# Loading w_o with four neighbouring rows to a partition in a fused decode layer, forward and backward

## The chip, the cores and the metric

The kernel runs on one core of one Trainium2 chip. The time is the device time of one execution in microseconds (us); the median of several executions is compared. A profile is one more execution, recorded by the hardware; its span is a little shorter than its own time, because start and end of the program lie around it.

## What is computed

One decoder layer with adaptive layer norm, for a single token of width 1024, and its gradients for all inputs. Attention has 32 query heads of 128 on 4 key/value heads and looks at the last 4096 of 65536 cached positions; the feed-forward network (FFN) is a gated unit of width 3584.

```python
mod = (silu(c) @ w_mod)              # sa, ca, ga, sb, cb, gb: six sections of 1024
h = layernorm(x) * (1 + ca) + sa
q = h @ wq                           # 32 heads of 128
p = softmax(q k^T * 128**-0.5)       # last 4096 positions of the cache
o = p v
x = x + ga * (o @ wo)                # wo: (32*128, 1024)
h = layernorm(x) * (1 + cb) + sb
x = x + gb * ((sigmoid(h @ w_gate) * (h @ w_up)) @ w_down)
```

The outputs are x and the gradients of x, k_cache, v_cache, wq, wo, w_gate, w_up, w_down, c and w_mod. The gradients of the two caches are zero outside the last 4096 positions, and writing these zeros is most of the memory traffic: 185.60 MB are written to memory and 78.28 MB read.

## The kernel before, in words

The order of the work is written out by hand; nothing is scheduled by a planner. Each engine runs its own list in order. Transfers are issued by POOL (most of them), by SP (w_down, parts of w_mod, some stores of the end) and, at the start, by ACT. The zeros go out as some 120 pieces of about 1 MB. `zero(n, after)` issues the next n of them on POOL; `after` makes POOL wait for a matmul first, so that the fills are paced by the computation. The lists `Z_...` at the top say how many are issued at which place. `dep` and `recent` only carry these waits.

The stages, with their times in the profile:

- Up to about 72 us: the loads of K, w_q and V, the modulation, q, the scores and the softmax. w_q is transposed into `A_all` (also called `a4[:, j, h, :]`: eight blocks j of 128 input rows, 32 heads h).
- The N loop, 72 to 155 us, line 697. For each of the four groups g of eight query heads it accumulates, over 32 steps t_, a 128x1024 matrix in two PSUM banks (`n_ps`, line 708), from keys times values weighted with p. One DVE product (line 703, in helper line 233) serves two steps, a *pair*. It ends with a rank-1 term (line 726, it needs `bd`, built by ACT in step 20) and two ACT copies into `N_sb` (line 729). At odd steps `side()` runs one waiting job.
- The jobs of groups 1 to 3 are the `t_unit`s (line 660) of the group before: T of head h is `N_sb` of the head, transposed, times the transposed w_q block of the head; two matmuls of 512 columns (line 666) and two copies (line 668) put it back into `a4`. The last eight heads (`tlast`) come after the loop, between the first chunks of b.
- b, 155 to 305 us: `bch()` (line 755) multiplies T of one input block p, four heads at a time, with the four 128-row blocks of one w_o tile `wo_t[u]`: eight matmuls into two banks (line 765). Between them: `attn_units` (o times w_o, line 787), the second layer norm, the folding of w_mod and the first loads of the FFN.
- The FFN, 306 to about 478 us: seven blocks q, each loaded, used for forward and backward, overwritten by its gradient and stored. In its idle moments PE transposes `wo_t` in place (line 1077), for do.
- The end: dattn (the gradient at the attention's output), do = w_o times dattn (line 1188, copied by ACT at line 1190 into `do_sb`, then turned into columns `do_ps` at line 1275), the gradient of w_o (`dwo`, line 1218), and those of w_mod, w_q, V and K.

w_o has 4096 rows: head times 128 plus position d in the head. `wo_t[u]` holds the 512 rows of heads 4u to 4u+3 as four tiles `[:, a, :]` of 128 partitions. In the loads (`wo_dram`, line 371) the tile index a is the head and the partition is d, so one partition takes four rows that are 128 rows apart in memory. In the store of its gradient (`dwo_dram`, line 374) a partition takes four rows that are neighbours. For that store, o is brought into the second order by 16 small fp32 matmuls (`op_ps`, line 1156), copied to `o_perm` (the buffer of `kb_col`), before the last layer norm's backward step.

PSUM has few banks; each pool names its own by a tag: `mm`, `gu`, `x`, `acc`, `pq`, `rq` one each, `na` two. `new_ps()` hands out banks in turn (in the N loop: `mm`, `gu`, `x`), `new_acc()` the bank `acc`.

Of the kernel before, what the change touches and what calls it, by code (L numbers as in the profile page):

```python
# [10 lines left out]
P = 128  # L11
FP32 = mybir.dt.float32
# [12 lines left out]
HQ = 32  # L25
G = 4
HG = HQ // G
DH = 128
# [18 lines left out]
NT = 8  # L47
# [12 lines left out]
def kernel(  # L60
# [26 lines left out]
    nc = tc.nc  # L87
# [3 lines left out]
    psum = ctx.enter_context(tc.tile_pool(name="psum", bufs=1, space=bass.MemoryType.PSUM))  # L91
    pacc = ctx.enter_context(tc.tile_pool(name="pacc", bufs=1, space=bass.MemoryType.PSUM))
    pna = ctx.enter_context(tc.tile_pool(name="pna", bufs=2, space=bass.MemoryType.PSUM))
    pgu = ctx.enter_context(tc.tile_pool(name="pgu", bufs=1, space=bass.MemoryType.PSUM))
    px = ctx.enter_context(tc.tile_pool(name="px", bufs=1, space=bass.MemoryType.PSUM))
# [25 lines left out]
    ident_f = vt([P, P], "ident_f")  # L121
# [96 lines left out]
    def new_ps(name="ps"):  # L218
        p, tag = next_pool()
        return p.tile([P, 512], FP32, name=name, tag=tag)  # L220
# [4 lines left out]
    def new_acc(name="acc"):  # L225
        return new_bank(name)[:, 0:64]
# [14 lines left out]
    def cp(out, a):  # L241
        return nc.vector.tensor_copy(out=out, in_=a)  # L242
# [110 lines left out]
    a4 = A_all.rearrange("p (j h m) -> p j h m", j=KD, h=HQ)  # L353
# [5 lines left out]
    N_sb = ar(144, 8)  # L359
# [6 lines left out]
    wo_t = [ar(o, 8).rearrange("p (a n) -> p a n", a=4) for o in wo_off]  # L366
# [2 lines left out]
    B_t = [junk if o is None else ar(o, 2) for o in B_off]  # L369

    def wo_dram(t, u):
        return t[u * 512:(u + 1) * 512, :].rearrange("(a d) n -> d a n", d=DH)

    def dwo_dram(u):
        return out_5[u * 512:(u + 1) * 512, :].rearrange("(p a) n -> p a n", a=4)

    def load_wo(u, eng=nc.gpsimd):
        eng.dma_start(out=wo_t[u], in_=wo_dram(A_wo, u))
# [123 lines left out]
    jobs = []  # L502
# [26 lines left out]
    for j in range(KD):  # L529
# [6 lines left out]
        for b in range(2):  # L536
            mm = rows_mm(q_ps[b], h1_bf[:, j:j + 1], heads(wq_t[j])[:, 16 * b:16 * b + 16, :], j == 0, j == KD - 1)
# [15 lines left out]
    for ch in range(8):  # L553
        ps = new_ps("sc_ps")
        for g in range(G):
            mm = nc.tensor.matmul(ps[32 * g:32 * g + 32, 0:512], lhsT=q_col2[:, HG * g:HG * g + 32],
                                  rhs=k_T[:, g, ch * 512:(ch + 1) * 512], start=True, stop=True,
                                  tile_position=(0, 32 * g))
# [18 lines left out]
    for tb in range(4):  # L577
        c = slice(tb * 1024, (tb + 1) * 1024)
# [31 lines left out]
    o_col = vt([P, HQ], "o_col")  # L610
    o_bf = vt([P, HQ], "o_bf", BF16)
    kb_col = vt([P, HQ], "kb_col")
# [26 lines left out]
    def ok_rows():  # L639
        cp(o_col, ok_ps[:, 0:HQ])  # L640
        cp(kb_col, ok_ps[:, HQ:2 * HQ])
        cp(o_bf, o_col)
        lo = scr[:, 768:832].bitcast(FP32)
        for k, (col, rows, s) in enumerate(((o_col, o_rows, 1.0), (kb_col, nkb_rows, -1.0))):
            st = st_cols[k].rearrange("p (a h) -> p a h", a=4)
            cp(st[:, 0, :], col)
            tt(lo, col, st[:, 0, :], ALU.subtract)
            cp(st[:, 3, :], lo)
            cp(st[:, 1, :], st[:, 3 - 3 * k, :])
            cp(st[:, 2, :], st[:, 3 * k, :])  # L650
            rp = new_tp("rp_ok")[:, 0:P]
            nc.tensor.transpose(rp, st_cols[k], ident_bf[:, :])
            nc.scalar.activation(out=rows, in_=rp, func=ACT.Copy, scale=s)

    def build_bd(g):
        for i in range(HG):
            nc.scalar.activation(out=bd[:, i, :], in_=o_rows, func=ACT.Copy,
                                 scale=sel[:, HG * g + i:HG * g + i + 1])

    def t_unit(h, engs="AA"):  # L660
        def run():
            for k in range(2):
                j1 = min(4 * k + 4, NT)
                ps = new_ps("t_ps").rearrange("p (j m) -> p j m", j=4)[:, 0:j1 - 4 * k, :]
                o = a4[:, 4 * k:j1, h, :]
                nc.tensor.matmul(ps, lhsT=N_sb[:, h * P:(h + 1) * P], rhs=o, start=True, stop=True)  # L666
                if engs[k] == "A":
                    nc.scalar.copy(out=o, in_=ps)  # L668
                else:
                    cp(o, ps)  # L670
        return run

    jobs.clear()

# [22 lines left out]
    for g in range(G):  # L697
        nbank = bank_pair("n_ps", g)
        for t_ in range(KT):
            s = g * KT + t_  # L700
            vp = vp_t[(s // 2) % 2]
            if t_ % 2 == 0:
                tt(vp.rearrange("p t h d -> p (t h d)"),
                   v_nat[:, g, t_ * DH:(t_ + 2) * DH].rearrange("p (t o d) -> p t o d", t=2, o=1).broadcast_to([P, 2, HG, DH]),
                   pT2[:, g, HG * t_:HG * t_ + 2 * HG, :].rearrange("p n (o k) -> p n o k", o=1).broadcast_to([P, 2 * HG, 64, 2]),
                   ALU.mult)
            for k in range(2):
                mm = nc.tensor.matmul(nbank[k][:, :], lhsT=k_nat[:, g, t_ * DH:(t_ + 1) * DH],  # L708
                                      rhs=vp[:, t_ % 2, 4 * k:4 * k + 4, :].rearrange("p h d -> p (h d)"),
                                      start=(t_ == 0), stop=False)  # L710
            zero(Z_N[s], recent(mm, 6), True)
            if t_ == 20:
                build_bd(g)
            if s == 2:
                ok_cols(ok4)
            elif s == 4:
                ok_rows()
            elif s == 24:
                gb_cols = mod_gb((6, 7))
                load_wo(0)  # L720
            elif s == 26:
                gb_cols()
            elif t_ % 2 == 1:
                side()
        for k in range(2):
            nc.tensor.matmul(nbank[k][:, :], lhsT=nkb_rows[:, :], rhs=bd[:, 4 * k:4 * k + 4, :].rearrange("p h d -> p (h d)"),
                             start=False, stop=True)
            c0 = (HG * g + 4 * k) * P
            nc.scalar.activation(out=N_sb[:, c0:c0 + 512], in_=nbank[k][:, :], func=ACT.Copy, scale=float(SCALE))
        load_wo(4 + g)  # L730
        if g < 3:
            jobs.extend(t_unit(h, "AA") for h in range(HG * g, HG * g + HG))
    load_wo(3)
    side(len(jobs))
    tlast = [t_unit(h, "AV") for h in range(HG * 3, HQ)]


    bq = []
# [36 lines left out]

    for i in range(4):
        bch()
        tlast[2 * i]()
        tlast[2 * i + 1]()
    bch(2)  # L780
    attn_col = vt([P, KD], "attn_col")
    row_sel = vt([P, 1], "row_sel")
# [1 line left out]
    attn4 = [new_ps("attn4") for _ in range(2)]  # L784

    def attn_units(us, first):
        for a in range(4):
            for k in range(2):
                for c in range(4):
                    h = 4 * us[c] + a  # L790
                    nc.tensor.matmul(attn4[k][32 * c:32 * c + 32, :], lhsT=o_bf[:, h:h + 1].broadcast_to([P, 32]),
                                     rhs=wo_t[us[c]][:, a, k * 512:(k + 1) * 512], start=(first and a == 0),
                                     stop=(not first and a == 3), tile_position=(0, 32 * c))

# [87 lines left out]
    v = A3_ps[:, 0:48].rearrange("p (j n) -> p j n", j=KD)  # L882
# [270 lines left out]
    dh2 = vt([P, KD], "dh2")  # L1153
    nc.vector.reduce_sum(out=dh2, in_=dh2acc.rearrange("p (b j) -> p j b", j=KD), axis=AX.X)
    dln2 = vt([P, KD], "dln2")
    op_ps = new_acc("op_ps")
    for hh in range(4):
        for a in range(4):
            nc.tensor.matmul(op_ps[32 * hh:32 * hh + 32, 8 * a:8 * a + 8], lhsT=ident_f[:, a::4], rhs=o_col[:, hh::4],
                             start=True, stop=True, tile_position=(0, 32 * hh))  # L1160
    o_perm = kb_col
    cp(o_perm, op_ps[:, 0:HQ])
    mulv(dln2, dh2, cb1)
    dx1b, m2 = layernorm_bwd_col(dln2, ln2, rstd2, "ln2b")
    dx1 = vt([P, KD], "dx1")
# [16 lines left out]
    do4 = [new_ps("do4") for _ in range(2)]  # L1182
    do_sb = [ar(158, 2).bitcast(FP32), scr.bitcast(FP32)]
    for b in range(2):
        for i in range(KD):
            for a in range(4):
                w = wo_t[4 * b + a].rearrange("p a (i d) -> p i a d", i=KD)
                nc.tensor.matmul(do4[b][32 * a:32 * a + 32, :], lhsT=dattn_bf[:, i:i + 1].broadcast_to([P, 32]),
                                 rhs=w[:, i, :, :], start=(i == 0), stop=(i == KD - 1), tile_position=(0, 32 * a))
        nc.scalar.copy(out=do_sb[b], in_=do4[b][:, :])  # L1190
    dh1_ps = new_acc("dh1_ps")
    for p in range(NBP):
        for it in range(KD):
            nc.tensor.matmul(dh1_ps[:, p:p + 1], lhsT=B_t[p][:, it * P:(it + 1) * P], rhs=dattn_bf[:, it:it + 1],
                             start=(it == 0), stop=(it == KD - 1))
# [22 lines left out]
    def dwo(u):  # L1218
        for a in range(4):
            outer_dve(wo_t[u][:, a, :], o_perm[:, 8 * a + u:8 * a + u + 1], dattn_b)  # L1220
        nc.gpsimd.dma_start(out=dwo_dram(u), in_=wo_t[u])

    def rebuild_P():
        tp = new_tp("tp_P")
# [48 lines left out]
    for b in range(2):  # L1273
        for hh in range(4):
            nc.tensor.matmul(dov[:, b, :, hh], lhsT=do_sb[b][:, hh * P:(hh + 1) * P], rhs=ident_f[:, 0::32],
                             start=True, stop=True)
    for g in range(G):
        tr_unit(N_sb[:, g * 1024:(g + 1) * 1024])()
    for u in (2, 4, 5, 6):
        dwo(u)  # L1280
# [25 lines left out]
    for tc_ in range(4):  # L1306
        nc.tensor.matmul(c_ps[32 * tc_:32 * tc_ + 32, 0:1], lhsT=pd, rhs=ones_f[:, 0:1],
                         start=True, stop=True, tile_position=(0, 32 * tc_))
# [17 lines left out]
    for c2 in range(2):  # L1326
        ps = new_ps("dp_ps")
# [107 lines left out]
```

## Time and profile before

| | |
|---|---|
| median of 3 runs | 594.28 us (593.79 to 594.58) |
| the profiled execution: its own time, its span | 593.98 us, 592.2 us |
| DMA bytes, mean rate over the span | 246.53 MB, 416 GB/s |
| share of DMA time on POOL's queue, on SP's and ACT's | 92.3%, 12.8% |
| packets under 8 KB, all packets | 23712, 37484 |
| 1 MB loads of w_o: number, median from issue to landing | 8, 11.4 us |
| 1 MB loads of w_q: number, median from issue to landing | 8, 20.9 us |
| T matmuls (line 666): number, ns of one | 64, 379 |
| T copies on ACT (line 668): number, ns of one | 56, 588 |

Busy time of an engine is given with its share of the span. A row of the profile's groups reads: line, engine, operation, what it writes <- what it reads, shape, number, then busy time and the mean length of one, then the idle time of the engine just before, with what ended it. Matmuls are pipelined: one of 512 columns is shown as 379 ns long, while the next can start 216 ns later. PEld is the load of a matmul's weights. A transfer's time to landing counts from its issue and includes waiting behind earlier ones. A line of a stretch of time (a window) gives its start and end, its length, the busy time and number of instructions of PE, PEld, DVE, ACT and POOL, the granted TensorE clock, the DMA share and GB/s.

### The profile page before, as it was taken

The page shows a single profiled execution, that of the slowest core. Times are in us where ns is not written, and L with a number is a line of the kernel's source. Part 1 is how long each engine was busy: PE and PEld are TensorE (multiplying, and loading weights), DVE is VectorE, ACT ScalarE, POOL GpSimd, SP SyncE. Part 2 cuts the span into 40 slices and gives each one's busy share as a digit, 9 for nine tenths or more (in the row PEclk, how much of TensorE's full clock was granted, in tenths as well). Part 3 has the DMA queues.
Part 4 walks back from the last instruction along what each step waited for, and adds up shares of the span by engine and source line. Part 5 has one row for each costly group of instructions (what it writes and reads, how often), then busy time and mean ns, then how long its engine had stood idle before and what let it go on. Part 6 is the DMA issues. An engine that isn't in the chain of part 4 may idle for free.

```text
span 592.2 us, 9529 instructions
## 1 busy us (share of the span) xinstructions
PE 397.7 (67%) x3819; PEld 239.4 (40%) x3844; DVE 360.7 (61%) x677; ACT 259.9 (44%) x398; POOL 158.0 (27%) x258
## 2 busy tenths in 40 slices
PE   3997689999899999988866237244262455984030
PEld 2784333334344546534436136234252424631000
DVE  3665599999511020176548685677866878968160
ACT  2579614567311014212135375464654655893020
POOL 3112223212223112222221334223343145222000
PEclk9998699999999999997995565565555568755555
DMA  8999999999999999999999999999999999999998
GB/s 349 420 419 421 412 457 388 464 417 430 426 422 396 431 446 424 432 431 401 421 422 388 417 414 416 409 413 416 416 414 413 419 419 405 419 425 420 422 416 363
DMA packets 37484, 246.53 MB, mean 416 GB/s; under 512 B 6097, under 2 KB 6097, under 8 KB 23712
## 3 DMA queue, kind: packets, MB, share of 16 engines
q0 software_dynamic: 30144, 218.65, 92.3%
q1 hardware_dynamic: 7248, 27.27, 12.8%
q8 instruction: 30, 0.49, 0.3%
q14 instruction: 14, 0.11, 0.1%
q10 hardware_dynamic: 48, 0.01, 0.0%
HBM read 78.28 MB, written 185.60 MB: 446 GB/s over the span
## 4 chain that ended last, share of the span: by engine, by line
DMA 36%; PE 34%; DVE 18%; ACT 5%; issue 4%; ACTq 0%; DVEq 0%; POOLq 0%; POOL 0%; SPq 0%
DMA out_dram<-arena 15%; PE b_ps L765 12%; DMA arena<-in_B_w_down_dram 7%; DMA out_dram<-out_dram 6%; PE n_ps L708 6%; DVE arena L246 5%; DVE arena L250 5%; DMA arena<-in_B_w_gate_dram 5%; DVE arena L233 4%; DMA arena<-in_w_mod_dram 3%; ACT arena L519 2%; PE t_ps L666 2%; PE w_ps L461 1%; PE tp_k L498 1%; PE tp_side L908 1%
## 5 line engine op out<-in xcount | busy, mean ns | idle before, releaser
L765 PE MATMUL b_ps<-arena 128*128 128x512 bf16 x494 | 116.0, 383 | 2.5 <-ACT arena L909 1.1
L909 ACT COPY arena<-tp_side 128x1024 bf16<-128x1024 bf16 x62 | 60.9, 1014 | 71.4 <-PE tp_side L908 71.1
L233 DVE TENSOR_TENSOR arena<-arena 128x2048 bf16<-128x2048 bf16 x64 | 76.5, 1223 | 2.3 <-PE n_ps L708 0.3
L765 PEld LDWEIGHTS <-arena 128*128 128x128 bf16 x512 | 49.2, 99 | 58.7 <-issue 5.3
L250 DVE CUSTOM_DVE_ANT_0 arena<-arena,scr 128x1024 bf16<-128x1024 bf16 x56 | 66.2, 1219 | 9.5 <-ACT scr L1071 9.5
L708 PE MATMUL n_ps<-arena 128*128 128x512 bf16 x249 | 65.2, 378 | 6.2 <-DVE arena L233 4.2
L200 POOL DMA_DIRECT2D out_dram<-out_dram x68 | 33.6, 495 | 116.2 <-PE n_ps L708 37.5
L908 PE MATMUL tp_side<-ident_bf,arena 128*128 128x128 bf16 x496 | 54.9, 289 | 11.6 <-DVE arena L233 5.2
L908 PEld LDWEIGHTS <-arena 128*128 128x128 bf16 x496 | 47.0, 135 | 17.6 <-issue 8.9
L1032 PE MATMUL fg<-h_bf,arena 128*128 128x1 bf16 x448 | 15.6, 166 | 48.3 <-DMA arena<-in_B_w_up_dram 28.8
L708 PEld LDWEIGHTS <-arena 128*128 128x128 bf16 x256 | 24.6, 97 | 41.2 <-issue 15.8
L250 DVE CUSTOM_DVE_ANT_0 arena<-arena,b1k 128x1024 bf16<-128x1024 bf16 x24 | 28.4, 1220 | 20.8 <-PE fg L1050 20.8
L281 ACT ACTIVATE arena<-scr,h 128x1024 bf16<-128x1024 bf16 x35 | 38.6, 1144 | 2.3 <-DVE dh2acc L250 1.5
L206 POOL DMA_DIRECT2D out_dram<-zeros x45 | 25.1, 562 | 54.0 <-PE q_ps L436 15.1
L941 POOL DMA_DIRECT2D out_dram<-arena x28 | 22.1, 793 | 64.4 <-ACT arena L281 45.4
L1255 ACT ACTIVATE arena<-ps_kv 128x512 bf16<-128x512 f32 x48 | 25.0, 723 | 29.7 <-PE ps_kv L1251 29.7
L1251 PE MATMUL ps_kv<-arena 32*128 32x512 bf16 x64 | 23.8, 543 | 19.7 <-DVE arena L246 18.6
L668 ACT CAST arena<-t_ps 128x512 bf16<-128x512 f32 x56 | 30.1, 588 | 12.1 <-PE t_ps L666 12.1
L242 DVE CAST arena<-b_ps 128x512 bf16<-128x512 f32 x6 | 4.1, 691 | 50.4 <-PE b_ps L765 50.4
L1032 PEld LDWEIGHTS <-arena 128*128 128x128 bf16 x448 | 14.0, 105 | 50.9 <-DMA arena<-in_B_w_up_dram 30.4
L519 ACT COPY arena<-tp_wq 128x1024 bf16<-128x1024 bf16 x23 | 21.4, 1071 | 7.3 <-PE tp_wq L517 7.3
L246 DVE TENSOR_SCALAR arena<-arena,cs_col 128x4096 bf16<-128x4096 bf16 (+1 forms) x16 | 16.0, 1014 | 12.3 <-DMA out_dram<-arena 12.3
(314 smaller groups left out, 618.1 us busy)
## 6 DMA issues: line engine op xcount, KB each, us to landing
out_dram<-zeros POOLq DMA_DIRECT2D x45, 1024.0 KB, 14.1
out_dram<-arena POOLq DMA_DIRECT2D x28, 1024.0 KB, 18.5
out_dram<-arena POOLq DMA_DIRECT2D x30, 512.0 KB, 10.9
out_dram<-arena SPq DMA_DIRECT2D x20, 512.0 KB, 9.8
arena<-in_A_wq_dram POOLq DMA_DIRECT2D x8, 1024.0 KB, 20.9
arena<-in_A_wo_dram POOLq DMA_DIRECT2D x8, 1024.0 KB, 11.4
arena<-in_w_mod_dram POOLq DMA_DIRECT2D x7, 1024.0 KB, 19.0
arena<-in_B_w_up_dram POOLq DMA_DIRECT2D x14, 512.0 KB, 12.2
```

The costliest lines, as they stand in the source:

```text
L200: ins = nc.gpsimd.dma_start(out=as_rows(region, BIGP).bitcast(FP32), in_=zero_src[:, 0:P * ZW // 4].rearrange("i (p x) -> (i p) x", p=BIGP ...
L233: return nc.vector.tensor_tensor(out=out, in0=a, in1=b, op=op)
L246: return nc.vector.tensor_scalar(out=out, in0=a, scalar1=s1, scalar2=None, op0=op0)
L250: return nc.vector.tensor_tensor_reduce(out=out, in0=w, in1=b, scale=1.0, scalar=0.0, op0=ALU.mult, op1=ALU.add, accum_out=acc)
L281: return nc.scalar.activation(out=out, in_=b, func=ACT.Copy, scale=col)
L519: nc.scalar.copy(out=blk, in_=tp[:, :])
L668: nc.scalar.copy(out=o, in_=ps)
L708: mm = nc.tensor.matmul(nbank[k][:, :], lhsT=k_nat[:, g, t_ * DH:(t_ + 1) * DH], rhs=vp[:, t_ % 2, 4 * k:4 * k + 4, :].rearrange("p h d -> ...
L765: mm = nc.tensor.matmul(bbank[p][k][:, :], lhsT=a4[:, p, h, :], rhs=wo_t[u][:, a, k * 512:(k + 1) * 512], start=(i == 0 and a == 0), stop= ...
L908: nc.tensor.transpose(tp[:, i * P:(i + 1) * P], blk[:, i * P:(i + 1) * P], ident_bf[:, :])
L909: nc.scalar.copy(out=blk if dst is None else dst, in_=tp[:, :])
L1032: nc.tensor.matmul(gu[:, col:col + 1], lhsT=ug_v[:, q % 2, j // 4, j % 4, k, f0:f0 + 255:2], rhs=h2_bf[:, j:j + 1], start=(j == 0 and i == ...
```

## The change

The loads of w_o take the order of the store: partition p of `wo_t[u]` holds rows 4p to 4p+3 of the 512, that is head 4u + p/32 (rounded down), positions 4(p mod 32) + a for a = 0 to 3. Everything that is multiplied with w_o along these rows follows:

- T: its rows have to come out in the same order. For a set of four heads u, half k of the input blocks and offset a, four matmuls with every fourth weight column (32 of them) of the four heads write the four quarters of one bank; `tile_position` gives each its own group of 32 columns of the array. Since all four a read all four heads and are then written over them, four banks (`mm`, `gu`, `x`, `acc`) are filled first and copied back after the fourth. Each (u, k, a) is a job of its own: 16 per group instead of eight.
- o: the shuffle by 16 matmuls moves from the end of the FFN to step 6 of the first group of the N loop; `o_bf`, which attn reads, is now made from the shuffled o there.
- attn reads column 8a + u in place of 4u + a.
- do: the copies out of PSUM write in the old order of positions.

```diff
     def wo_dram(t, u):
-        return t[u * 512:(u + 1) * 512, :].rearrange("(a d) n -> d a n", d=DH)
-
-    def dwo_dram(u):
-        return out_5[u * 512:(u + 1) * 512, :].rearrange("(p a) n -> p a n", a=4)
+        return t[u * 512:(u + 1) * 512, :].rearrange("(p a) n -> p a n", a=4)
...
         cp(kb_col, ok_ps[:, HQ:2 * HQ])
-        cp(o_bf, o_col)
...
+    o_perm = kb_col
+
+    def shuffle_o():
+        op_ps = new_acc("op_ps")
+        for hh in range(4):
+            for a in range(4):
+                nc.tensor.matmul(op_ps[32 * hh:32 * hh + 32, 8 * a:8 * a + 8], lhsT=ident_f[:, a::4], rhs=o_col[:, hh::4],
+                                 start=True, stop=True, tile_position=(0, 32 * hh))
+        cp(o_perm, op_ps[:, 0:HQ])
+        cp(o_bf, o_perm)
...
-    def t_unit(h, engs="AA"):
+    t_pools = ((psum, "mm"), (pgu, "gu"), (px, "x"), (pacc, "acc"))
+    t_banks = []
+
+    def t_unit(u, k, a, engs="AAAA"):
         def run():
-            for k in range(2):
-                j1 = min(4 * k + 4, NT)
-                ps = new_ps("t_ps").rearrange("p (j m) -> p j m", j=4)[:, 0:j1 - 4 * k, :]
-                o = a4[:, 4 * k:j1, h, :]
-                nc.tensor.matmul(ps, lhsT=N_sb[:, h * P:(h + 1) * P], rhs=o, start=True, stop=True)
-                if engs[k] == "A":
-                    nc.scalar.copy(out=o, in_=ps)
+            pl, tag = t_pools[a]
+            ps = pl.tile([P, 512], FP32, name="t_ps", tag=tag)
+            t_banks.append(ps)
+            for hh in range(4):
+                h = 4 * u + hh
+                nc.tensor.matmul(ps[32 * hh:32 * hh + 32, :].rearrange("p (j m) -> p j m", j=4),
+                                 lhsT=N_sb[:, h * P + a:(h + 1) * P - 3 + a:4], rhs=a4[:, 4 * k:4 * k + 4, h, :],
+                                 start=True, stop=True, tile_position=(0, 32 * hh))
+            if a < 3:
+                return
+            for i in range(4):
+                o, v = a4[:, 4 * k:4 * k + 4, 4 * u + i, :], t_banks[i].rearrange("p (j m) -> p j m", j=4)
+                if engs[i] == "A":
+                    nc.scalar.copy(out=o, in_=v)
                 else:
-                    cp(o, ps)
+                    cp(o, v)
+            t_banks.clear()
         return run
+
+    def t_units(g, engs="AAAA"):
+        return [t_unit(u, k, a, engs) for u in (2 * g, 2 * g + 1) for k in range(2) for a in range(4)]
...
             elif s == 4:
                 ok_rows()
+            elif s == 6:
+                shuffle_o()
...
-            jobs.extend(t_unit(h, "AA") for h in range(HG * g, HG * g + HG))
+            jobs.extend(t_units(g))
...
-    tlast = [t_unit(h, "AV") for h in range(HG * 3, HQ)]
+    tlast = t_units(3, "AVAV")
...
     for i in range(4):
         bch()
-        tlast[2 * i]()
-        tlast[2 * i + 1]()
+        for run in tlast[4 * i:4 * i + 4]:
+            run()
...
-                    h = 4 * us[c] + a
-                    nc.tensor.matmul(attn4[k][32 * c:32 * c + 32, :], lhsT=o_bf[:, h:h + 1].broadcast_to([P, 32]),
+                    n = 8 * a + us[c]
+                    nc.tensor.matmul(attn4[k][32 * c:32 * c + 32, :], lhsT=o_bf[:, n:n + 1].broadcast_to([P, 32]),
...
-        nc.scalar.copy(out=do_sb[b], in_=do4[b][:, :])
+        nc.scalar.copy(out=do_sb[b].rearrange("q (h r a) -> q a h r", h=4, a=4),
+                       in_=do4[b].rearrange("q (a h r) -> q a h r", a=4, h=4))
...
-        nc.gpsimd.dma_start(out=dwo_dram(u), in_=wo_t[u])
+        nc.gpsimd.dma_start(out=wo_dram(out_5, u), in_=wo_t[u])
```

## The prediction

> **What bounds the kernel now.** I read the page's slices first, then the stretches of the one load that changes, then the waits of POOL, the chain of waits, and the start and landing of single transfers in the trace. The page:
>
> ```profile
> span 592.2 us, 9529 instructions
> PE 397.7 (67%) x3819; PEld 239.4 (40%) x3844; DVE 360.7 (61%) x677; ACT 259.9 (44%) x398; POOL 158.0 (27%) x258
> ...
> DMA  8999999999999999999999999999999999999998
> ```
>
> No engine is busy all the time, but the 16 DMA engines are: 9 tenths or more in every slice but the first and last. 246.53 MB at a mean of 416 GB/s is the span. The waits of POOL, which issues 92.3% of the DMA time, say how that comes about, from 60 to 176 us and from 176 to 306 us:
>
> ```profile
> POOL out_dram L200 <- PE n_ps L708: 37.5, 19, 3.2
> POOL out_dram L200 <- PE t_ps L666: 15.2, 7, 4.1
> ...
> POOL out_dram L200 <- DMA out_dram<-out_dram: 27.3, 16, 2.1
> ```
>
> Until 176 us the zero fills are paced by PE; afterwards POOL mostly waits for one of its own earlier transfers (it has eight landing semaphores in turn, so at most eight are under way). The chain of waits agrees; from 250 us it runs through whole queues:
>
> ```profile
> 250.40 18.96 DMA out_dram<-out_dram
> 269.64 17.14 DMA out_dram<-out_dram
> 287.32 19.13 DMA arena<-in_w_mod_dram
> 306.50 0.86 PE g_ps L436 x24
> ```
>
> A 1 MB fill takes 2.43 us when the next lands behind it, so 19 us to landing is a queue of some 16 us. The time is therefore DMA work, plus what the engines idle. A later PE costs nothing while a queue stands. It first costs where the queue is shortest.
>
> **The load.** Rows of w_o are 2 KB; the eight 1 MB loads (L378) fetch four separate ones per partition, afterwards one run of 8 KB. The loads of 22 to 46 us (w_q, v) have such 8 KB runs, and 66 to 70 us holds w_o loads almost alone:
>
> ```profile
> 22.00:46.00 24.00, 23.02 (x392) 19.67 (x388) 17.05 (x30) 15.07 (x19) 2.64 (x5) 1.00 1.01 419
> 66.00:70.00 4.00, 3.06 (x26) 2.09 (x27) 1.79 (x7) 1.55 (x6) 2.16 (x4) 0.50 1.04 395
> ```
>
> The last column is GB/s. 8 loads x 1.049 MB = 8.39 MB: 21.2 us at 395, 20.0 us at 419, so 1.2 us less; packet times say the same (4 KB packets of w_o at 165.6 ns, 8 KB packets of w_q and v at 314.7 ns: 2.65 against 2.52 us per MB, 1.1 us in all). I take **-1.1**. Bounds: 2 KB-row loads of w_mod between fills cost as little as 2.51 us each, against the 2.49 us between landings of w_q: -0.2; the two w_o loads issued at 156 us, with the edges to the fills around them, cost 2.89 each: -3.2. POOL's issue falls from 795 to 542 ns, hidden, since POOL waits anyway.
>
> The Trainium skill, "DMA: Bandwidth & Descriptors", section "Specifications", speaks against the gain: transfers from 512 B up run at line rate. By it 2 KB is as good as 8 KB and this term is 0; the rows above (395 against 419) disagree.
>
> **T by column groups.** Before, there are 64 matmuls of 128 weight columns (L666); 16 each run in groups 1 to 3 of the N loop, two in each of the first eight of a group's 16 pairs of steps. Such a pair lasts 1.296 us (six matmuls at 0.216: starts 119.64, 120.94, 122.23), and 1.20 in the other eight, where the DVE product sets the pace. After, 256 matmuls of 32 columns, one set of four in each of the 16 pairs. Sets of four exist in the trace, at attn:
>
> ```profile
> 178.68 1.03 PE L765 MATMUL b_ps<-arena 128*128 128x512 bf16 x4
> 179.64 1.91 PE L791 MATMUL attn<-arena,o_bf 128*32 128x512 bf16 x32
> 181.71 0.59 PE L765 MATMUL b_ps<-arena 128*128 128x512 bf16 x2 [0.16 <-issue]
> ```
>
> 32 of them, starting within 1.53 us, step at 0.216 per four: they do run side by side. Going in costs 179.64 - (178.68 + 4 x 0.216) = 0.10. Going out looks like 0.33, but two weight loads stand ahead of the first b_ps matmul shown, so one record is probably missing and it is 0.10. A set then costs 0.216 + 0.2 = 0.41 and a pair 0.864 + 0.41 = 1.28. Per group 16 x 1.28 - 8 x (1.296 + 1.20) = +0.5, three groups **+1.5 us of PE lateness**; with the dear exit +0.23 x 48 = +11 more; if the switch hid behind the DVE wait, 16 x 1.20, -0.8 a group, -2.3.
>
> Four matmul sets now fill four banks before four ACT copies run back to back (they start 0.49 apart and take 0.59). The last set of a group is in its last pair, and the two N_sb copies (L729) queue behind these four on ACT:
>
> ```profile
> 135.19 0.59 PE L726 MATMUL n_ps<-arena,scr 128*128 128x512 bf16 x2
> ...
> 135.61 1.08 ACT L729 ACTIVATE arena<-n_ps 128x512 bf16<-128x512 f32 x2 [6.10 <-PE n_ps L726]
> ...
> 136.49 0.59 PE L666 MATMUL t_ps<-arena 128*128 128x512 bf16 x2
> ```
>
> Today ACT has been idle 6.1 us there. Afterwards, from the last set's start: copies from 0.41, the N_sb copy 2.37 to 2.96, the next group's first set wants it at 0.31 + 0.43 + 0.86 + 0.10 = 1.7. PE, and the N matmuls and pacing fills behind it, wait 1.3 us at two group starts and 0.4 before the last units (one b chunk of 1.73 stands between): **+3.0**. The last units: four rounds of 12 matmul times plus two switches, 11.2 us, against 12.1 from 155.49 to 167.6: **-0.9**.
>
> **Shuffle of o**, moved from the end of the FFN to step 6 of group 0: 16 fp32 matmuls in two passes, 32 records of 1.45 us in all at L1159, and two small DVE copies behind them (0.18 each), one of which left step 4. In the DVE-paced loop the next product waits: **+1.4**, bounds 0.5 and 2. At its old place 0.10 leaves the chain (kb_col L242); the queue of 6 us there hides it. Sum on PE: 1.5 + 3.0 - 0.9 + 1.4 = **5 us late** at 167 us (-2 to +16).
>
> **The copies of do** (L1190) now write with a step of four floats: 0.59 each today, twice that at worst. do_ps would end at 490.96 + 1.2, before DVE reads it at 492.72 behind twelve outer products: 0. attn only renames columns: 0. The dwo stores keep their layout: 0.
>
> **More PE instructions.** 0.49 MB of instruction fetch in 30 packets for 7663 PE records is 64 B each; 384 more are 25 KB, 1.5 packets of about 1 us, on one engine perhaps: 0.1 to 1.5, **+0.3**.
>
> **What 5 us cost.** PE is 92.8 of 95 us busy from 155 to 250, so the delay stays until the FFN begins at 306. The cover is the queue. It is shortest at 331.57, where a 512 KB store lands after 9.2 us: 8 us ahead of it on the last engine. The 16 counts of a landing come 5.1 us apart there (336.96 to 342.05), mean 2.95, so the mean engine has 8 - 2.15 = 5.85 us, the earliest 2.9. Lateness 5 and DMA sooner by 1.1 use 6.1: some engines idle, on the mean 0.3, the early ones over 3 us, part of which they idle today at 497.5 to 499.5 us (1.3 engines of 16 there). I take **+0.5**. Later rounds recover: DVE is busy 121.3 of 165 us from 315 to 480, and the w_down transfers of 10 us on the chain shorten with the queue.
>
> Sum: -1.1 + 0.3 + 0.5 = **-0.3** on the profiled execution (span 592.2, 593.98 with what lies around it), that is 593.7; on the median of 594.28, **594.0**, no change that can be told.
>
> **Rivals.**
> (a) Faster: PE is hardly late (switches hide, or the fast engines' idle is what they have anyway) and the whole DMA gain shows. Between 1.1 and half the upper bound: -1.6, **592.7**. For it: the saturated DMA row; and the chain is DMA from 250 us on. Against: PE runs without a pause from 155 us.
> (b) Slower: the lateness breaks the queue at the start of the FFN. The place is the boundary of the groups and the switches; at 8.5 us late (a going-out cost of 0.17) 8.5 + 1.1 - 5.85 = 3.7 us of DMA idle, less 0.8: +2.9, **597.2**. It decides from about 7 us on. For it: the four copies ahead of N_sb are certain; against: the pairs have 0.2 us of PE wait in the second half.
> The Trainium skill, "TensorEngine Tiling (Array Packing)", section "Key Properties", supports this rival: changing the tiling mode drains TensorE. A full drain here would be 379 - 216 ns at each switch, 0.54 a set, some 6 us later than my sum; the 0.10 going in at attn speaks for less.
> (c) No gain from long runs at all, lateness as in the sum, with less of the queue used: +0.3 + 0.2, **594.8**. For it: the w_mod loads at 2.51 us; against: 395 beside 419 GB/s. This is also what the Trainium skill's "Specifications" rule cited above gives.
>
> **How the numbers follow.** About 0.2% (1.2 us) can be told from no change. Forecast 0.35 (its own range 593.0 to 595.3), (a) 0.30, (b) 0.30, (c) 0.05. Nearly all of (a) counts as faster, of (b) as slower; a tenth of the forecast lies on the faster side: faster 0.29, within 0.2% 0.38, slower 0.33. The range reaches to (b) and past (a): 592.0 to 597.8; left out are the full upper load gain and the dear exit.
>
> **What would show it.** w_o windows at 415 GB/s or more; four T matmuls starting within 10 ns, and pairs of 1.28 us in groups 1 to 3; ACT L729 waiting on nothing and PE waiting for it twice; b_ps starting about 5 us later than 155.49; transfers to landing near 331 us well under 9 us. Wrong if PE's lateness is outside 2 to 8 us, if the w_o loads keep 395 GB/s, or if the DMA slices of the FFN fall under 9.

## The result, and the profile after

The changed kernel takes 600.48 us (median of 5 runs, 600.16 to 602.6) against 593.98 us of the kernel before beside it (593.79 to 594.58): a ratio of 1.0116, 95% interval 1.0105 to 1.0128. It is 1.2% slower. The profiled execution has 600.48 us itself and a span of 598.7.

The head of the page after, and its rate in 40 slices of 15 us:

```profile
span 598.7 us, 9909 instructions
...
PE 405.1 (68%) x4007; PEld 236.0 (39%) x4036; DVE 362.5 (61%) x677; ACT 259.3 (43%) x398; POOL 153.7 (26%) x258
...
DMA  8999999999999999999999999999999999999997
GB/s 348 422 420 419 423 458 374 451 440 435 422 413 379 464 427 388 451 422 427 371 412 372 357 411 415 405 409 417 414 415 412 418 418 412 423 424 425 424 416 321
```

PE is 7.4 us busier. The DMA row is as full as before, because its digit stops at 9 and a slice holds 15 us. The row below it is finer: slices 22 and 23 (314 to 344 us) carry 372 and 357 GB/s, where before they carry 388 and 417. That is the start of the FFN.

What POOL waits for, from 60 to 176 us and from 176 to 306 us, in the kernel after:

```profile
POOL out_dram L200 <- PE n_ps L729: 54.7, 24, 4.6
...
POOL out_dram L200 <- PE b_ps L788: 48.3, 21, 5.3
POOL arena L378 <- PE b_ps L788: 17.1, 5, 5.1
...
POOL out_dram L200 <- DMA arena<-in_w_mod_dram: 1.3, 1, 1.3
```

This is the clearest sign in the profile. Between 176 and 306 us, POOL before waited mostly for its own earlier transfers, 27.3 us for copies of zeros alone: the queue was full. After, it waits for PE's b matmuls: PE is so late that the queue drains while b runs; the 1 MB loads of w_mod land after a median of 12.2 us, 19.0 before. The bill comes at the start of the FFN. Two stretches of 6 us there (the last three columns are the granted TensorE clock, the DMA share and GB/s), first before, then after:

```profile
320.00:326.00 6.00, 4.74 (x88) 4.34 (x88) 5.86 (x12) 5.81 (x7) 0.14 (x1) 0.50 1.23 420
338.00:344.00 6.00, 4.47 (x51) 4.08 (x52) 5.17 (x12) 3.22 (x4) 3.65 (x5) 0.50 1.12 424
```

```profile
320.00:326.00 6.00, 2.61 (x93) 2.47 (x90) 5.52 (x13) 1.23 (x3) 0.56 (x1) 0.50 0.86 324
338.00:344.00 6.00, 3.73 (x56) 3.30 (x55) 5.69 (x13) 3.25 (x4) 4.17 (x6) 0.50 0.75 272
```

420 GB/s fall to 324 and 272. Estimated from the starts and lengths of the single packets, the mean DMA engine is idle for 2.74 us between 320 and 360 us, against 0.03 before. (The trace does not name a packet's engine; these estimates, here and below, are good to a few tenths of a us.)

Where the 6.5 us of span went, per mean engine and by the same estimate: idle ahead of 580 us grew from 2.7 to 6.0 us (+3.3, of it 2.7 here and 0.6 at 176 to 200 us); the wait of early engines for the last one at the end grew from 1.9 to 3.5 (+1.6); the packets themselves took 1.6 us longer, although those of w_o became shorter. The last two are less sure: over four executions with a full queue (before, and in the experiments the load alone, 4.1 us of PE and both edits) the wait at the end varies from 1.9 to 2.5 us, and the time in packets by 2.6 us.

**Where PE became late.** The N loop runs from the first `n_ps` matmul to the first `b_ps` matmul: 74.36 to 155.49 us before, 72.03 to 164.19 after, so 81.13 against 92.16, **11.0 us longer**. It began 2.3 us sooner in this execution, mostly because the granted clock was full again from 67.4 us instead of 72.4 (the 64 `ok` matmuls ahead of the loop take 3.64 us instead of 5.13), so that the FFN's first store is only 8.25 us later than before (323.60 against 315.35). By group, from one rank-1 term to the next:

| | before | after | difference |
|---|---|---|---|
| group 0 (the shuffle) | 21.10 | 24.78 | +3.7 |
| group 1 (T sets) | 19.86 | 21.44 | +1.6 |
| groups 2 and 3, each (T sets, boundary) | 19.87 | 22.75 | +2.9 |
| first `b_ps` to attn (last units) | 24.15 | 23.91 | -0.2 |

The boundary of groups 1 and 2, PE and then ACT, in the kernel after:

```profile
117.90 0.41 PE L677 MATMUL t_ps<-arena 128*32 128x512 bf16 x4
118.25 0.60 PE L749 MATMUL n_ps<-arena,scr 128*128 128x512 bf16 x2
118.69 1.03 PE L729 MATMUL n_ps<-arena 128*128 128x512 bf16 x4
120.95 0.41 PE L677 MATMUL t_ps<-arena 128*32 128x512 bf16 x4 [1.24 <-ACT arena L752]
122.26 0.41 PE L677 MATMUL t_ps<-arena 128*32 128x512 bf16 x4
```

```profile
118.34 2.05 ACT L685 CAST arena<-t_ps 128x512 bf16<-128x512 f32 x4 [3.20 <-PE t_ps L677]
120.26 1.13 ACT L752 ACTIVATE arena<-n_ps 128x512 bf16<-128x512 f32 x2
```

The set at 120.95 needs the new `N_sb`; its copies start on ACT only after the four T copies. The next set comes 1.31 us later: that is the length of a pair with a set in it.

### The profile page after: what moved, and what is told of

It is laid out like the page before. It is cut to its first block, busy times and chain, and to the rows that moved or that the text cites. A ratio compares the mean times of both kernels' runs of the same rounds, so it can differ in the third digit from the quotient of the medians.

```text
span 598.7 us, 9909 instructions
## 1 busy us (share of the span) xinstructions
PE 405.1 (68%) x4007; PEld 236.0 (39%) x4036; DVE 362.5 (61%) x677; ACT 259.3 (43%) x398; POOL 153.7 (26%) x258
## 5 line engine op out<-in xcount | busy, mean ns | idle before, releaser
L233 DVE TENSOR_TENSOR arena<-arena 128x2048 bf16<-128x2048 bf16 x64 | 77.7, 1224 | 9.0 <-PE n_ps L729 4.0
L788 PEld LDWEIGHTS <-arena 128*128 128x128 bf16 x512 | 48.9, 99 | 57.8 <-issue 5.0
L931 PEld LDWEIGHTS <-arena 128*128 128x128 bf16 x496 | 47.1, 135 | 19.2 <-issue 10.3
L685 ACT CAST arena<-t_ps 128x512 bf16<-128x512 f32 x56 | 28.9, 598 | 39.9 <-PE t_ps L677 39.9
L729 PEld LDWEIGHTS <-arena 128*128 128x128 bf16 x256 | 21.4, 99 | 35.8 <-issue 19.5
L1055 PEld LDWEIGHTS <-arena 128*128 128x128 bf16 x448 | 13.8, 105 | 51.0 <-DMA arena<-in_B_w_up_dram 30.8
L677 PE MATMUL t_ps<-arena 128*32 128x512 bf16 x256 | 24.1, 399 | 3.4 <-ACT arena L752 2.8
## 6 DMA issues: line engine op xcount, KB each, us to landing
arena<-in_w_mod_dram POOLq DMA_DIRECT2D x7, 1024.0 KB, 12.2
```

Of the source, the lines that this page charges most:

```text
L233: return nc.vector.tensor_tensor(out=out, in0=a, in1=b, op=op)
L685: nc.scalar.copy(out=o, in_=v)
L788: mm = nc.tensor.matmul(bbank[p][k][:, :], lhsT=a4[:, p, h, :], rhs=wo_t[u][:, a, k * 512:(k + 1) * 512], start=(i == 0 and a == 0), stop= ...
L931: nc.tensor.transpose(tp[:, i * P:(i + 1) * P], blk[:, i * P:(i + 1) * P], ident_bf[:, :])
L1055: nc.tensor.matmul(gu[:, col:col + 1], lhsT=ug_v[:, q % 2, j // 4, j % 4, k, f0:f0 + 255:2], rhs=h2_bf[:, j:j + 1], start=(j == 0 and i == ...
```

## Experiments

The kernel before ran beside each of them, at 594.34 to 594.36 us.

**The load alone, and the change without it.** First the kernel before with only the loads of w_o in the new order:

```diff
     def wo_dram(t, u):
-        return t[u * 512:(u + 1) * 512, :].rearrange("(a d) n -> d a n", d=DH)
+        return t[u * 512:(u + 1) * 512, :].rearrange("(p a) n -> p a n", a=4)
```

> The kernel before with one edit: the w_o loads take four neighbouring rows to a partition. T, o and do keep the old order, so attn and do multiply rows that do not belong together; the amount of work is unchanged. If the slowdown of the change is lateness of PE (theory L), this is 0.7 to 1.3 us faster than before, with the w_o stretch near 415 GB/s. If the new load order is itself slow (theory D: the DMA engines were active 1.6 us longer after the change though fewer packets were moved), it is 1 to 6 us slower. If runs of 2 KB were as good as 8 KB, within 0.3 us.

593.6 us (592.96 to 593.77), ratio 0.9985 [0.9976, 0.9994]: 0.9 us gained by the ratio (0.7 between the medians). The opposite, the changed kernel with its loads back in the old order:

```diff
     def load_wo(u, eng=nc.gpsimd):
-        eng.dma_start(out=wo_t[u], in_=wo_dram(A_wo, u))
+        eng.dma_start(out=wo_t[u], in_=A_wo[u * 512:(u + 1) * 512, :].rearrange("(a d) n -> d a n", d=DH))
```

> The changed kernel with one edit: the w_o loads alone go back to rows 128 apart, so attn and do again multiply rows that do not belong together. Theory L: b still starts about 8 us late and the time is 0.7 to 1.3 us above the changed kernel, about 601.5. Theory D: the time falls back to within 1 us of before, 593 to 595.

601.15 us (600.27 to 602.7), ratio 1.0113 [1.0089, 1.0137]. The slowdown stays; it isn't in the loads.

**Lateness alone.** Does a late PE cost this by itself? The kernel before with 38 further matmuls (8.2 us of PE, their result not used) behind the N loop, and then with 19 of them:

```diff
+    idle_ps = new_ps("idle_ps")
+    for i in range(38):
+        nc.tensor.matmul(idle_ps, lhsT=ident_bf[:, :], rhs=v_nat[:, 3, 0:512], start=True, stop=True)
     bq = []
```

> The kernel before with 38 added matmuls of 512 columns (8.2 us of PE, result unused) between the N loop and the last T units; nothing else. Theory L: about the lateness of the change without its cheaper loads, so DMA engines idle at the start of the FFN and the time is 598 to 602. If the queue hides 8 us of lateness, the time stays within 0.6 us of before and the slowdown of the change has another cause.

> The kernel before with 19 further matmuls of 512 columns (4.1 us of PE) between the N loop and the last T units, half the dose of the kernel with 8.2 us. Theory L with the cover as read (mean engine 5.85 us, earliest 2.9): the FFN starts 4.1 us later, hardly any engine is idle for it: 594.3 to 596.0, of 4.1 us at most 1.5 come back in the time. Rival (no threshold: each us of lateness costs the same as in the kernel with 8.2 us, 4.8 of 8.2): 596.7.

8.2 us of PE: 599.16 us (596.69 to 599.57), ratio 1.0072 [1.0049, 1.0094], +4.8 us. Half of it: 594.56 us (593.7 to 596.1), ratio 1.0005 [0.9996, 1.0014], nothing that can be told. The price is not in proportion: it has a threshold between the two. Not all of the smaller dose reaches the FFN: its first store is issued 2.7 us later than before (318.07), with 8.2 us it is 7.5 (322.89). With 8.2 us, the same two stretches show the same hole as the changed kernel:

```profile
320.00:326.00 6.00, 1.49 (x38) 1.42 (x38) 5.52 (x17) 0.24 (x2) 0.56 (x1) 0.50 0.92 344
338.00:344.00 6.00, 3.73 (x56) 3.30 (x55) 5.68 (x15) 3.03 (x4) 4.30 (x6) 0.59 0.79 277
```

With 4.1 us they are full:

```profile
320.00:326.00 6.00, 4.67 (x89) 4.34 (x90) 4.62 (x12) 4.00 (x5) 1.05 (x2) 0.50 1.14 425
338.00:344.00 6.00, 4.38 (x50) 3.99 (x51) 4.53 (x12) 3.12 (x4) 3.35 (x6) 0.50 1.12 421
```

No instruction of the change is in these two kernels, so lateness of PE is enough to cause most of the loss.

**The shuffle, placed elsewhere.** First in the changed kernel between the last T units and the next b chunk:

```diff
-            elif s == 6:
-                shuffle_o()
...
         for run in tlast[4 * i:4 * i + 4]:
             run()
+    shuffle_o()
     bch(2)
```

> The changed kernel with the shuffle of o moved from step 6 of the N loop to the place after the last T units, before attn. Theory L: the first group wins back the 3.7 us it lost, b starts some 5 us late, and the time falls by 2.5 to 4 us, to 596.5 to 598, since each us of lateness beyond the queue costs one. If lateness is not the cause, the time stays within 0.6 us of the changed kernel.

601.85 us, but with a spread from 598.54 to 602.91; ratio 1.0116 [1.0084, 1.0148]. A miss: in the profiled execution (598.54 us) group 0 takes 21.03 us, as before the change, but at the new place the shuffle takes 2.9 us of PE without a pause to absorb it: 1.41 waiting for DVE to empty the `acc` bank and 1.46 of its own. Removing 3.7 us of lateness and adding 2.9 tells little; that the median is 1.4 us above the changed kernel's, with a little less lateness, stays unexplained.

Then in step 12 of group 0, where bank and data have long been ready, with its copies on ACT instead of DVE:

```diff
-        cp(o_perm, op_ps[:, 0:HQ])
-        cp(o_bf, o_perm)
+        nc.scalar.copy(out=o_perm, in_=op_ps[:, 0:HQ])
+        nc.scalar.copy(out=o_bf, in_=o_perm)
...
-            elif s == 6:
+            elif s == 12:
                 shuffle_o()
```

> The changed kernel with only the shuffle moved to step 12 and its two copies on ACT; T sets one at a time, as in the changed kernel. Theory L: the shuffle's 3.7 us of PE lateness, with the window of half clock, fall away; the sets' lateness of 6.5 to 7 us at the end of the N loop, beside the kernel that only loads w_o in the new order, stays. No idle in 72 to 100 us, and 0.5 to 2 us of engine idle in 320 to 360: 595 to 597.5. Rival S (the shuffle and the half clock behind it are the whole cause): 593.5 to 594.5. Rival T (the sets alone make the whole loss, the shuffle is hidden): 600 to 601.

599.1 us (598.39 to 599.88), ratio 1.0085 [1.0068, 1.0102]: 1.4 us less than the changed kernel, above the range expected. Group 0 takes 22.53 us, so the shuffle costs 1.4 us of PE here instead of 3.7 (its place and the engine of its copies were changed together, so their shares are not known). The sets alone are more than the cover holds: the mean engine still idles 2.15 us between 320 and 360.

**T sets two at a time.** The same matmuls and copies; only one way into and out of the 32-column mode for two sets:

```diff
-            elif t_ % 2 == 1:
-                side()
+            elif t_ % 4 == 1:
+                side(2)
```

> The changed kernel with its T sets taken two at a time, in every fourth step instead of one in every second; the same matmuls and copies. Theory L (PE's lateness breaks the queue at the start of the FFN): one way into and out of the 32-column mode in two pairs instead of two, so two pairs take 2.40 us (DVE's pace) instead of 2 x 1.313: 1.8 us less a group, 5.4 in three; the last set is two steps earlier, so the N_sb copies hardly wait: 1.2 us less at each of two boundaries. The end of the N loop comes 6 to 8 us sooner than in the changed kernel, inside the cover, and the time is 594 to 596. Rival D (the time went into the DMA traffic itself or behind the FFN: the do copies, the instruction fetch, the w_o rows): unchanged, 600 to 601.

595.66 us (593.55 to 596.68), ratio 1.0018 [1.0004, 1.0031]: 4.8 us less than the changed kernel. Its N loop takes 86.68 us, 5.5 less: 1.2 in each of groups 1 to 3 by the sets, 0.9 more at each of the two boundaries. The same boundary in this kernel, two sets (eight matmuls) in a row:

```profile
118.88 0.59 PE L749 MATMUL n_ps<-arena,scr 128*128 128x512 bf16 x2
119.31 1.03 PE L729 MATMUL n_ps<-arena 128*128 128x512 bf16 x4
120.71 0.63 PE L677 MATMUL t_ps<-arena 128*32 128x512 bf16 x8 [0.37 <-ACT arena L752]
```

The wait of 1.24 us has become 0.37. The queue at 320 us holds (417 GB/s from 320 to 326). Some is lost elsewhere: this execution entered the N loop late (73.99 us) and still has the shuffle in step 6, and from 84 to 96 us it carries 350 GB/s, against 419 in the kernel before. So there is a second place where the queue can break.

Both edits together:

> The kernel with two sets at a time, and the shuffle of o in step 12 instead of 6 with its two copies on ACT. There the acc bank and o_col have long been ready, and DVE's product queue isn't held up: PE's 1.45 us go into the 0.33 us that each pair of group 0 leaves it. Theory L: shuffle's 3.7 us of lateness fall to 0 to 1, the granted clock keeps 1.0 at 81 to 85 us; the end of the N loop within 2 us of that of the kernel that only loads w_o in the new order; time 593.3 to 594.8, the gain of the load shows at last. Rival D: 600. If the shuffle costs nothing beside what the two sets at a time save, the same as the kernel with two sets alone.

593.72 us (593.42 to 594.95), ratio 0.9996 [0.9986, 1.0005]. The N loop takes 84.52 us. Between 176 and 306 us POOL still waits for PE, but less than half as long as in the changed kernel, and again for its own transfers; the stretches at the start of the FFN are full:

```profile
POOL out_dram L200 <- PE b_ps L788: 21.7, 10, 3.1
POOL out_dram L200 <- DMA out_dram<-out_dram: 17.9, 11, 2.2
```

```profile
320.00:326.00 6.00, 4.78 (x90) 4.29 (x89) 5.53 (x10) 5.82 (x7) 0.47 (x1) 0.50 1.21 418
338.00:344.00 6.00, 4.87 (x56) 4.39 (x57) 4.03 (x10) 3.62 (x4) 3.52 (x5) 0.54 1.11 421
```

This kernel does all that the change does, the 256 small matmuls, the copies of do and the new loads included. Together the rest costs little here: by the interval, this kernel lies between 0.8 us under and 0.3 us over the kernel before, and the load alone gains 0.9, so at most some 1.2 us are left for it. So the loss of some 6 us goes with PE's lateness. This is the fastest of the versions that hold the whole change; it can't be told from the kernel before, nor from the one with the load alone.

**More queue instead of less lateness.** Three fills of 1 MB go out ahead of the FFN instead of in its last two rounds; in the changed kernel, and as a control in the kernel before:

```diff
-Z_FOLD = (1, 1, 1, 2)
+Z_FOLD = (2, 3, 1, 2)
-Z_FFN = [(0, 2, 0, 2), (0, 2, 0, 1), (0, 2, 0, 2)] + [(0, 2, 0, 2)] * 2 + [(1, 1, 1, 3), (1, 2, 1, 0)]
+Z_FFN = [(0, 2, 0, 2), (0, 2, 0, 1), (0, 2, 0, 2)] + [(0, 2, 0, 2)] * 2 + [(1, 1, 1, 1), (1, 1, 1, 0)]
```

> The changed kernel, with three 1 MB zero fills issued ahead of the start of the FFN instead of in its last two rounds; nothing on PE, ACT or DVE differs. Theory L: PE is as late as in the changed kernel (end of the N loop at 160 to 164 us), but the queue at the start of the FFN is 7.3 us longer, so engines do not idle there (2.7 us in 320 to 360 today, under 0.5 then); the time is 595.5 to 598, what is left being the uneven end of the 16 engines. Rival D, or PE's lateness acting through the chain itself and not through the queue: 600 to 601.

> Control: the kernel before with the same three fills moved. Theory L: its queue never ran empty, so there is nothing to gain: 594.0 to 595.0 (a little more where the moved fills leave the end of the FFN with less to do). Rival: fills at an earlier place are better in themselves, then 592 or less, and the fill-moving run on the changed kernel says nothing on the queue.

The changed kernel: 598.86 us (596.87 to 600.14), ratio 1.0073 [1.0051, 1.0095], above the range expected. The control: 595.6 us (595.18 to 597.47), 1.0029 [1.0018, 1.0041], a miss too, since it was expected at no loss. In the changed kernel the hole is filled (408 and 418 GB/s, idle 0.04 us from 320 to 360), although PE is just as late. But the fills are missed where they came from (1.5 us of idle between 480 and 500 us in the control, 0.9 in the other), and the profiled execution, the slowest of its four, lost 2.56 us at 72 to 100 us. Of the 6.1 us between the medians (600.48 and 594.36), 1.6 come back; against the control, the change costs 3.3 us. So the hole is a matter of the queue, but in these two kernels moving fills moved the thin place too.

## Why the prediction was wrong

The forecast was no change, 594.0; measured 600.48, above the range. The mechanism, a late PE that the queue covers up to a point, was in the text. Two terms of the sum were too small: how late PE gets (5 us against 10.8), through the T sets and the shuffle, and what lateness beyond the cover costs.

- **The load, -1.1: right.** The load alone gives -0.9 (-1.4 to -0.4 by the interval), and the stretch of w_o loads goes from 395 to 422 GB/s, with w_q's at 418 (over all profiled executions 394 to 397 in the five with the old order, 421 to 429 in the seven with the new):

```profile
22.00:46.00 24.00, 23.02 (x391) 19.68 (x389) 16.44 (x30) 15.33 (x19) 2.65 (x5) 1.00 1.01 418
...
66.00:70.00 4.00, 3.06 (x43) 2.06 (x46) 2.62 (x9) 1.66 (x10) 2.12 (x4) 0.83 1.02 422
```

  The rule cited against it (the Trainium skill, "DMA: Bandwidth & Descriptors", "Specifications": line rate from 512 B up) does not hold to the last 6% here, as the two rates show.
- **"A set then costs ... 0.41 and a pair ... 1.28": the first step that failed, three times too small as a sum.** A set costs 1.313 - 0.864 = 0.45, a little more than thought. The larger error was the old loop: the 16 pairs of a group were put at 8 x 1.296 + 8 x 1.20 = 19.97 us, but a group without its rank-1 term took 19.87 - 0.43 = 19.44. The second eight pairs took 9.07 us, 1.13 each, not the 1.20 read off the spacing of the DVE products. So +1.6 a group in place of +0.5. A full drain at each switch (the Trainium skill, "TensorEngine Tiling (Array Packing)", "Key Properties") was worked out as 0.33 for the two switches of a set (0.54 with its matmuls); they measure 0.45 - 0.22 = 0.23, so the trace shows a cost, but less than that estimate.
- **The boundaries, 1.3 us at two starts: right** (1.24 of wait each, for the reason given). The last units, -0.9 + 0.4, measured -0.2.
- **"Shuffle of o ... +1.4, bounds 0.5 and 2": failed, 3.7.** The 1.45 us of matmuls were right. Behind them PE waits for the DVE product, which the two small copies hold up, and then the granted clock is halved for 3.4 us (the last section); how the other 2.3 us divide between the two was not separated. The kernel with the shuffle in step 12 shows 1.4, about the matmuls alone. PE in the kernel after:

```profile
77.92 1.45 PE L657 MATMUL op_ps<-o_col,ident_f 128*32 128x8 f32 x32
79.53 0.38 PE L729 MATMUL n_ps<-arena 128*128 128x512 bf16 x1 [0.16 <-issue]
81.00 4.44 PE L729 MATMUL n_ps<-arena 128*128 128x512 bf16 x12 [1.09 <-DVE arena L233]
```

- **Sum: 5 us late predicted, 10.8 measured** (3.7 + 1.6 + 2.9 + 2.9 - 0.2 = 10.9; 11.0 over the N loop). That is past the 8 us at which the text called itself wrong.
- **"What 5 us cost", +0.5: not tested at 5, too small beyond.** The nearest dose, 4.1 us, costs +0.2 (-0.2 to +0.8), though only 2.7 us of it reach the FFN: "the delay stays until the FFN begins" was not quite so, for in the kernel before the FFN's start waits for a w_mod load (the chain shows it at 306.50). For 8.5 us late the text foresaw 2.9 us, and the 8.2 us of further matmuls cost 4.8. The idle itself was not foreseen too small: 3.7 us there, 2.74 in the changed kernel. The place was only half found: the text took the store of 331.57 us as the thinnest one. In the changed kernel the first hole opens ahead of the fills and stores of 323.6 to 323.87 us, the second ahead of that store. The price left out that the engines then wait longer for the last one at the end (+1.6, less the scatter named above); that packets took longer in sum (+1.6) may be scatter, and the rest of the price stays open.
- **Rival (b) was the right mechanism**, and its turning point of about 7 us lies within the measured bounds: 4.1 us of further matmuls are free, as are 3.4 us of longer N loop (both edits); 8.8 us of it (only the shuffle moved, to step 12) cost 4.7. Its time of 597.2 was too small by the price above. It was given 0.30, for want of the group length.
- **The copies of do, 0: right.** They take 1.16 us in place of 0.59, and DVE still reads `do_ps` behind its outer products:

```profile
490.49 1.16 ACT L1206 COPY arena<-do 128x512 f32<-128x512 f32 x1 [5.70 <-PE do L1204]
```

  One more packet of instructions (31 for 30) is too small to be told in the time.
- **The sign by which it would be seen was too coarse:** the DMA digits of the FFN stay at 9. Windows of 6 us show it.

## What to carry to other kernels

Where transfers bound a kernel and another engine paces their issue, that engine's lateness can be free up to what the thinnest place of the queue covers, and then the time follows it (4.1 us cost 0.2 here, 8.2 us 4.8): add up the lateness per loop from the start of one group to the start of the next, not from the pace of single pairs. Work that switches PE's mode can be cheaper in longer runs (two sets at a time took 1.2 us off a group here), and a bank of PSUM or an engine that the loop needs anyway should not be held by a side job's copies.

## What the runs showed of the hardware

**A stretch of small matmuls was followed by half the clock.** The 3.4 us ahead of the shuffle, the 3.4 us around it and the two stretches behind it, after the change; the third column from the end is the granted clock:

```profile
74.20:77.60 3.40, 2.06 (x10) 0.70 (x11) 2.97 (x14) 1.33 (x6) 0.53 (x1) 1.00 1.14 424
77.60:81.00 3.40, 2.15 (x36) 1.57 (x35) 1.56 (x4) 1.55 (x6) 0.52 (x1) 1.00 1.14 424
81.00:84.50 3.50, 3.50 (x9) 1.31 (x9) 2.31 (x2) 0.00 (x0) 0.00 (x0) 0.51 1.38 529
84.50:88.00 3.50, 2.94 (x13) 1.07 (x12) 3.40 (x3) 0.00 (x0) 0.98 (x2) 1.00 1.01 419
```

Around the shuffle PE is busy 2.15 of 3.40 us, of which 1.45 in matmuls of eight columns, and the next 3.5 us run at 0.51: nine matmuls of 512 columns fill them. The three other executions with the shuffle in step 6 (the old load order, two sets at a time, fills earlier) show the drop too, for 3.4, 3.4 and 6.8 us. A low busy share alone did not do it: the stretch of 74.20 us is busy for only 2.06, without such small matmuls, and the clock behind it stays at 1.00. With the shuffle in step 12 and the sets in twos, the 3.4 us with the same 32 matmuls are busy for 3.31, and the clock stays at 1.00 too:

```profile
80.70:84.10 3.40, 3.31 (x40) 1.99 (x40) 1.95 (x2) 1.42 (x6) 0.50 (x1) 1.00 1.38 528
```

The Trainium skill ("TensorE: Matmul & The Clock Gate", "Why this matters for your kernels") advises against idle gaps of PE over some 3 us; here the longest is 1.09 us, and the clock fell all the same. It would fit that the small matmuls count for little: what PE did beside them was 0.7 us here and up to 1.2 in the other three stretches before a drop, 1.5 and more in the two executions with the shuffle in step 12. No run tests that by itself.

**The clock changes on a grid of 3.41 us, with a phase of its own.** In all twelve profiled executions the granted clock keeps a value for a whole multiple of 3.41 us, but where the grid lies differs: the full clock comes back at 67.39 us in the changed kernel and at 72.37 in the kernel before, with the same work ahead of it. The first N matmul starts at 72.03 and at 74.36, in other executions at 71.8 to 74.5. A full queue can hide that (before: 593.7 to 595.2 over all runs). Where the queue runs empty, it may be part of the spread (598.5 to 602.9 with the shuffle behind the N loop); with one profiled execution of each kernel, this is not shown.
